# A linear-attention and GEGLU block in f32: how the first two tiles of x are loaded, and when the masks are made

## The chip, the cores and the metric

One core of a Trainium2 chip runs the whole kernel. The metric is the device time in microseconds (us) of one execution; the time of a version is the median of its runs.

## The reference

One block over a sequence of 2048 rows of width 576, all in f32. `x` is normalized by rows; the normalized rows go into a linear attention with 32 heads of 18 and into a gated feed-forward net of width 4608; the two results are multiplied and added to `x`.

```python
def block(x, wqkv, wo, w_gate, w_up, w_down):
    xn = (x - mean(x)) / sqrt(var(x) + 1e-5)
    q, k, v = heads(xn @ wqkv)                    # 32 heads of 18
    phi = lambda t: where(t > 0, t + 1, exp(t)) + 1e-6
    kv = einsum("bhsd,bhse->bhde", phi(k), v)     # over all rows
    z = phi(k).sum over s
    o = einsum(phi(q), kv) / (einsum(phi(q), z) + 1e-6)
    s = o @ wo
    h = gelu(xn @ w_gate) * (xn @ w_up)
    return x + s * silu(h @ w_down)
```

## The kernel before

The 2048 rows are 16 tiles of 128, in 4 blocks (`TB`) of 4 tiles (`TT`). A value of f32 is split into two fp32r words: ACT copies it to fp32r (the high word), and DVE or POOL subtracts that copy from the value (the low word). A product in full precision is then several passes of TensorE (PE) over words: `KV_PASSES` has seven for each of the two halves of the 576 columns.

The work in order: k and v (and the last columns of q) for all tiles, with `kv` summed up in PSUM; q; the normalizer and the attention's output matrix; then gate and up by blocks of columns; last the down product. From the second block of 8 tiles on, `x` comes in already transposed and is normalized in that form. The first four tiles are loaded with rows on partitions, normalized and transposed on PE.

The opening goes by a hand-written order, since `pin` keeps instructions of each engine as the program has them (helpers `act`, `vec`, `mm`, `pool`, `dma`; a line such as L90 or L87 in the profile is that of a helper). Calls on `nc.gpsimd` that are not pinned may be moved by the scheduler.

- `turn_idle(n, v)`: n transposes of `ident` (or of a small value, once that is there) into the PSUM tile `idle`, whose contents nobody reads. They stand at the beginning and in the gaps of the opening.
- `load_x(n, k, eng)`: a load of k row tiles of `x` into `x_n`, on SP's queue, or on that of `eng`. One tile is 384 KB.
- `load_kv(c, j)`: a piece of the k and v weights into `rw`, on SP's queue: 624 KB, or 576 KB for c = 2.
- `spread(n, k)`: the moments of a tile: on DVE two `bn_stats`, one `bn_aggr` and an addition, on ACT a Ln and an Exp. `scales(n)`: three small operations on DVE. `center(n)`: DVE subtracts the mean and multiplies by the scale, 128x768 in one instruction.
- `turn(n)`: six transposes of the normalized tile on PE, three for each half j, into the PSUM tiles `xt`. `place(n, js, words)`: ACT rounds `xt` into the operand `xo_B` (word 0), DVE writes the remainders (word 1).
- `kv_hi`, `kv_lo`: the two words of a weight piece into `wkv`, by ACT and by POOL or DVE. `x_mm(t, c, passes)`: the passes of tile t and weight piece c.

Two loads stand at the head of the queues: tile 0 on SP's, tile 1 on ACT's. Behind tile 0, SP's queue has the weight pieces and tiles 2 and 3. `make_masks` writes three things into `small`: `mask` and `maskh`, by `affine_select` on POOL, and `zc`, of which rows 64 to 127 are zeroed by a memset. It is called after tile 5 of the first pass. Its instructions are not pinned; in the program the scheduler has put the memset of `zc` ahead of the select that makes `ident`, and the others where the call stands. `mask`, `maskh` and `zc` are first read behind the sixteenth tile, at about 187 us.

Of the kernel before, what the change touches and what calls it, by code (L numbers as in the profile page):

```python
# [10 lines left out]
AF = mybir.ActivationFunctionType  # L11
ALU = mybir.AluOpType
# [3 lines left out]
P = 128  # L16
# [3 lines left out]
H = 32  # L20
DH = D // H
# [4 lines left out]
TT = TBN // P  # L26
NG = DF // (2 * P)
HG = 7
GW = HG * DH
NHG = 5  # L30
# [5 lines left out]
Q4 = 64  # L36
# [19 lines left out]
def block_kernel(ctx, tc, x, xe, xt_d, wq_d, wkv0_d, wkv1_d, wkv2_d, wo, wgu_d, wd_d, out):  # L56
    nc = tc.nc
# [11 lines left out]
    def big(i, shape, dt, name):  # L69
        return sb.tile(shape, dt, tag=f"b{i}", bufs=1, name=name)  # L70
# [10 lines left out]
    def tmp(shape, name):  # L81
        return sb.tile(shape, F32, tag="tmp", bufs=4, name=name)
# [3 lines left out]
    def act(*args, **kw):  # L86
        pin(nc.scalar.activation(*args, **kw))  # L87

    def vec(op, *args, **kw):
        pin(getattr(nc.vector, op)(*args, **kw))  # L90
# [4 lines left out]
    def pool(op, *args, **kw):  # L95
        pin(getattr(nc.gpsimd, op)(*args, **kw))  # L96

    def dma(out, in_, eng=None):
        tc.keep_in_program_order((eng or nc.sync).dma_start(out=out, in_=in_))
# [9 lines left out]
    small = sb.tile([P, 640], F32, name="small")  # L109
# [9 lines left out]
    def load_x(n, k, eng=None):  # L119

        if n % 2 == 0:
            xstat[n // 2] = big(14 + n // 2 % 2, [P, 12 * P], F32, f"x_{n}")
        if n < TT:
            o = x_of(n)[:, None] if k == 1 else xstat[n // 2][:, 0 : 12 * P].rearrange(
                "p (t j d) -> p t j d", t=2, j=2)
            dma(out=o, in_=xe[n * P : (n + k) * P].rearrange("(t p) j d -> p t j d", p=P), eng=eng)
        else:
            dma(
                out=xstat[n // 2][:, 0 : 2 * D].rearrange("p (t d) -> p t d", t=2),
                in_=x[n * P : (n + 2) * P].rearrange("(t p) d -> p t d", p=P),  # L130
            )

    def x_of(n):

        w = 6 * P if n < TT else D
        return xstat[n // 2][:, n % 2 * w : (n % 2 + 1) * w].rearrange("p (j d) -> p j d", j=2)
# [24 lines left out]
    def scales(n0):  # L161

        n, mv, st = mom.pop(n0)
        far = n0 >= TT
        v, r, c = (st[:, i, 0:n] for i in range(1, 4))
        if n == 1:
            vec("tensor_scalar", c, r, r, -0.5, op0=ALU.mult, op1=ALU.mult)
            vec("tensor_scalar", c, c, v, 1.5, op0=ALU.mult, op1=ALU.add)
            vec("tensor_scalar", c, c, r, None, op0=ALU.mult)
        else:  # L170
            vec("scalar_tensor_tensor", c, r, -0.5, r, op0=ALU.mult, op1=ALU.mult)
            vec("tensor_mul", c, c, v)
            o = mv[:, 0:n, 1] if far else c
            vec("scalar_tensor_tensor", o, c, 1.5, r, op0=ALU.add, op1=ALU.mult)
        if far:
            mom[n0] = mv
            return
        for t in range(n):
            scale_of[n0 + t] = mv[:, t, 0:1], c[:, t : t + 1]

    def center(n):

        xs = x_of(n)
        m, r = scale_of.pop(n)
        vec("tensor_scalar", xs, xs, m, r, op0=ALU.subtract, op1=ALU.mult)

    def spread_out(n):

        mr[n] = bank(f"mr_{n}")
        mv = mom.pop(n)  # L190
        for t in range(2):
            for q in range(2):
                o = mr[n][:, (2 * t + q) * P : (2 * t + q + 1) * P]
                pin(nc.tensor.transpose(o, mv[:, t, q : q + 1].to_broadcast([P, P]), ident))

    def norm(n, js=(0, 1)):

        tb, t = divmod(n, TT)
        s, b = divmod(tb, 2)
        v = mr[n].rearrange("p (t q c) -> p t q c", t=2, q=2)  # L200
        for j in js:
            f = xf[s][BS[b][j]][:, :, t * P : t * P + P2].rearrange("p k (t c) -> p k t c", t=2)
            for q, op in enumerate(("tensor_sub", "tensor_mul")):
                vec(op, f, f, v[:, None, :, q, :].to_broadcast([P, 3, 2, P]))
# [38 lines left out]
    mom, scale_of, xts, mr = {}, {}, {}, {}  # L243
# [54 lines left out]
    def load_kv(c, j):  # L298
        n = KV.index((c, j))
        if n % 2 == 0:  # L300
            raws["kv", n // 2] = big((2, 3, 12)[n // 2], [P, 2, 3, CW[c]], F32, f"rw_{n}")
        raws[c, j] = raws["kv", n // 2][:, n % 2]
        dma(out=raws[c, j], in_=wkv_d[c][j])
# [28 lines left out]
    def load_q(j):  # L332
        raws["q", j] = big(12, [P, 2, 3, Q2], F32, f"rq_{j}")
        dma(out=raws["q", j], in_=wq_d[:, j].rearrange("c p k f -> p c k f"))

    def prep_q(c, j):
        raw, main = raws["q", j][:, c], wq[j]
        cs, r = slice(c * Q2, (c + 1) * Q2), slice(2 * KR, 3 * KR)
        act(main[:, 0:3, cs], raw, AF.Copy)
        for o, src, hi in (  # L340
            (main[:, 3, cs], raw[:, 0, :], main[:, 0, cs]),
            (wq_l[:, j, cs], raw[:, 1, :], main[:, 1, cs]),
            (main[r, 2, cs], raw[r, 2, :], main[r, 2, cs]),
        ):
            pool("tensor_sub", o, src, hi.bitcast(F32))
# [183 lines left out]

    at = {}  # L530

    def band(m, src, pattern, c):
        nc.gpsimd.affine_select(
            out=m, in_=src, compare_op=ALU.is_ge, fill=0.0, base=0,
            pattern=[[-s, n] for s, n in pattern], channel_multiplier=c,
        )
        nc.gpsimd.affine_select(
            out=m, in_=m, compare_op=ALU.is_ge, fill=0.0, base=DH - 1,
            pattern=[[s, n] for s, n in pattern], channel_multiplier=-c,
        )  # L540

    def make_masks():
        ones = tmp([P, NHG * H], "ones")
        nc.gpsimd.memset(ones, 1.0)

        at["mask"] = mask = small[:, 0:GW]
        m3, o3 = (i.rearrange("p (h j) -> p h j", h=HG) for i in (mask, ones[:, 0:GW]))
        nc.gpsimd.affine_select(
            out=m3, in_=o3, compare_op=ALU.is_ge, fill=0.0, base=-1,
            pattern=[[-DH, HG], [0, DH]], channel_multiplier=1,  # L550
        )
        nc.gpsimd.affine_select(
            out=m3, in_=m3, compare_op=ALU.is_ge, fill=0.0, base=DH,
            pattern=[[DH, HG], [0, DH]], channel_multiplier=-1,
        )
        nc.gpsimd.memset(mask[0:1, :], 1.0)
        at["maskh"] = small[:, P : P + NHG * H].rearrange("p (g h) -> p g h", g=NHG)
        band(at["maskh"], ones.rearrange("p (g h) -> p g h", g=NHG), [[-GW, NHG], [DH, H]], 1)
        at["zc"] = small[:, P + NHG * H : P + 2 * NHG * H].rearrange("p (g h) -> p g h", g=NHG)
        nc.gpsimd.memset(at["zc"][Q4:P], 0.0)  # L560

    def kv_done():

# [561 lines left out]
    def turn_idle(n, v=None):  # L1125
        src = ident if v is None else v.to_broadcast([P, P])
        for _ in range(n):
            pin(nc.tensor.transpose(idle[:, 0:P], src, ident))

    turn_idle(20)  # L1130
    load_x(0, 1)
    load_kv(0, 0)
    load_x(1, 1, nc.scalar)
    load_kv(0, 1)
    load_kv(1, 0)
# [6 lines left out]
    spread(0, 1)  # L1142
    turn_idle(2, mom[0][1][:, 0, 0:1])
    scales(0)
    turn_idle(4, scale_of[0][1])
    center(0)
    turn(0, lambda n: (own_bank if n[-1] == "0" else bank)(n))
    turn_idle(3)
# [64 lines left out]
    def x_next(n):  # L1213

        spread(n, 2)
        scales(n)

    def form(nm, tb, j):

        o = build(0, nm, 12)  # L1220
        load_turned(tb, j)
        keep(0, nm, o)
# [19 lines left out]
    for n in range(3, 2 * TT):  # L1242
        early, middle, ends, after = [], [], [], []
        if n == 3:
            early += [lambda: spread_out(4), lambda: norm(4)]
        if n == 3:
            after.append(lambda: x_next(6))
        if n == 4:
            middle.append(lambda: spread_out(6))
            after.append(lambda: norm(6))  # L1250
        if n >= TT:
            j, c = divmod(n - TT, 2)
            prep_q(c, j)
            if n == TT + 1:
                load_q(1)
        if n == 5:
            after.append(lambda: x_next(8))
        if n == 6:
            after += [lambda i=i: difference(0, i) for i in range(2)]
        if n == 7:  # L1260
            ends.append(lambda: difference(0, 2))
            after.append(lambda: form("T1", 2, 0))
        kv_tile(n, early, middle, ends, after)
        if n in (4, 5):
            load_x(2 * n, 2)
        if n == TT:
            for nm in BS[0]:
                keep(0, nm, xo[0][nm])
        if n == TT + 1:
            make_masks()  # L1270
        if n == TT + 3:
            keep(0, "B22", xo[0]["B22"])

# [87 lines left out]
    for q in range(NQ):  # L1361
        g = q // 2
# [72 lines left out]
```

## Time and profile before

| what | value |
|---|---|
| median of 3 runs | 1493.03 us (1492.82 to 1493.14) |
| profiled execution | 1492.64 us |
| its span, first to last instruction | 1490.9 us |
| mean granted clock of TensorE | 0.999 |
| PE busy | 1482.9 us, 99% of the span |
| DVE, ACT, POOL busy | 1062.4, 563.4, 549.4 us |
| DMA | 260.67 MB, mean 175 GB/s |

Times in the views are from the span's start. "PE" is TensorE's matmuls (transposes too), "PEld" its weight loads; "SPq" and "ACTq" are the sequencers of SP and ACT that issue DMAs. In the chain and in the timeline a row has start, duration, engine or DMA, and what; in brackets stands how long the engine was idle before and what ended that. A row with "x6" is a group of six.

### The profile page before, as it was taken

To read this page: it belongs to the slowest core of one execution; us is meant where nothing else is said; L and a number is where in the kernel's file an instruction comes from. 1 tells how busy PE (TensorE), PEld (TensorE's weight loads), DVE (VectorE), ACT (ScalarE), POOL (GpSimd) and SP (SyncE) were. 2 spreads that over 40 slices of the span, in tenths; PEclk is the share of its full clock that TensorE was granted. 3 is DMA by queue.
4 is the path that set the end of the run, shared out by engine and by line. 5 is a ranking of instruction groups with operands and counts; after the bars stand their busy time and mean duration, and the time that the engine had idled before them with its cause. 6 is when DMAs were issued, how large, how long until landed. Compare 5 with 4: busy or idle time off the path is not lost.

```text
span 1490.9 us, 22327 instructions
## 1 busy us (share of the span) xinstructions
PE 1482.9 (99%) x8355; PEld 1328.2 (89%) x8355; DVE 1062.4 (71%) x1582; ACT 563.4 (38%) x1047; POOL 549.4 (37%) x521
## 2 busy tenths in 40 slices
PE   9999999999999999999999999999999999999998
PEld 8989989988888888888888888888899999999998
DVE  7678467377788787788787778787785575555775
ACT  5444455332232232332222322223445454445443
POOL 5453431144665544565554565554310020001120
PEclk9999999999999999999999999999999999999999
DMA  6355015533443423344433344333697666686873
GB/s 238 131 198 194 1 45 191 207 149 136 161 173 145 161 107 132 148 174 157 152 121 122 142 173 171 139 136 117 218 334 256 227 217 222 226 290 218 299 254 112
DMA packets 114614, 260.67 MB, mean 175 GB/s; under 512 B 10234, under 2 KB 38778, under 8 KB 112458
## 3 DMA queue, kind: packets, MB, share of 16 engines
q1 hardware_dynamic: 112730, 249.95, 46.7%
q0 software_dynamic: 1632, 8.91, 1.6%
q8 instruction: 65, 1.06, 0.3%
q10 hardware_dynamic: 144, 0.39, 0.1%
q14 instruction: 43, 0.35, 0.1%
HBM read 161.27 MB, written 97.91 MB: 174 GB/s over the span
## 4 chain that ended last, share of the span: by engine, by line
PE 95%; DVE 2%; DMA 1%; ACT 1%; POOL 0%; issue 0%; SPq 0%; DVEq 0%; ACTq 0%; POOLq 0%
PE bd L1010 27%; PE al L804 15%; PE ga L804 15%; PE de L804 15%; PE be L804 8%; PE kv L93 7%; PE s L93 4%; PE q L93 2%; PE kv_a L93 1%; DMA kept_T<-xo_T 1%; DMA xf_B<-in_xt_dram 0%; PE d L93 0%; PE kw L93 0%; DVE xf_B L90 0%; PE b L93 0%
## 5 line engine op out<-in xcount | busy, mean ns | idle before, releaser
L1010 PEld LDWEIGHTS bd<-t,s 128*128 128x128 f32 x3024 | 400.9, 188 | 0.1
L1010 PE MATMUL bd<-t,s 128*128 128x288 f32 x3024 | 401.0, 295 | 0.0
L90 DVE TENSOR_TENSOR s<-sr,s 128x512 fp32r<-128x512 f32 x252 | 176.4, 738 | 119.6 <-ACT s L87 110.1
L87 ACT ACTIVATE s<-sr 128x512 fp32r<-128x512 f32 x252 | 149.2, 625 | 189.6 <-PE bd L1010 133.6
L96 POOL TENSOR_TENSOR hs<-h,h 128x512 f32<-128x512 f32 x68 | 94.7, 1402 | 202.7 <-DVE h L90 200.0
L87 ACT ACTIVATE h<-h 128x512 f32<-128x512 f32 x108 | 67.1, 633 | 244.3 <-POOL sm L96 123.1
L96 POOL TENSOR_TENSOR sx<-sx 128x288 f32<-128x288 f32 x24 | 27.8, 1180 | 322.9 <-DVE sx L90 321.9
L93 PE MATMUL kv<-wkv,xo_B 128*128 128x416 f32 (+1 forms) x672 | 129.2, 349 | 0.3 <-DVE xo_B L90 0.2
L93 PEld LDWEIGHTS kv<-wkv,xo_B 128*128 128x128 f32 x672 | 121.6, 188 | 2.1 <-DVE xo_B L90 0.5
L96 POOL TENSOR_TENSOR sm<-raw 128x384 f32<-128x384 f32 x72 | 75.7, 1051 | 108.8 <-DMA raw<-in_wgu_dram 87.9
L90 DVE TENSOR_TENSOR wa<-raw,wa 128x256 fp32r<-128x256 f32 x72 | 79.0, 1098 | 51.6 <-ACT wa L87 50.5
L90 DVE TENSOR_TENSOR h<-h,u 128x512 f32<-128x512 f32 x108 | 95.7, 886 | 3.7
L87 ACT ACTIVATE wa<-sm 128x1152 fp32r<-128x1152 f32 x36 | 41.8, 1161 | 135.2 <-PE de L804 135.2
L96 POOL TENSOR_TENSOR td<-td 128x288 f32<-128x288 f32 x72 | 71.5, 993 | 50.9 <-DMA td<-in_wd_dram 46.6
L90 DVE TENSOR_TENSOR wa<-sm,wa 128x768 fp32r<-128x768 f32 x72 | 62.9, 874 | 36.9 <-ACT wa L87 36.0
L90 DVE TENSOR_TENSOR wb<-raw,wb 128x256 fp32r<-128x256 f32 (+1 forms) x108 | 72.0, 666 | 7.2 <-ACT wb L87 5.6
L90 DVE TENSOR_TENSOR wb<-sm,wb 128x256 fp32r<-128x256 f32 x72 | 61.5, 855 | 20.6 <-ACT wb L87 20.0
L87 ACT ACTIVATE u<-al 128x512 f32<-128x512 f32 x72 | 40.8, 593 | 88.4 <-PE al L804 88.4
L90 DVE TENSOR_TENSOR u<-u,ga 128x512 f32<-128x512 f32 x72 | 49.3, 686 | 19.8 <-PE ga L804 19.2
L804 PE MATMUL al<-xo_B,wa 128*128 128x512 f32 x252 | 63.0, 389 | 0.0
L804 PE MATMUL be<-xo_T,wa 128*128 128x512 f32 x252 | 63.0, 389 | 0.0
L804 PE MATMUL be<-xr_T,wa 128*128 128x512 f32 x252 | 63.0, 389 | 0.0
(175 smaller groups left out, 2779.1 us busy)
## 6 DMA issues: line engine op xcount, KB each, us to landing
sr<-hs SPq DMA_DIRECT2D x252, 256.0 KB
hs<-h SPq DMA_DIRECT2D x68, 512.0 KB
raw<-in_wgu_dram SPq DMA_DIRECT2D x36, 768.0 KB
hs<-hs SPq DMA_DIRECT2D x102, 256.0 KB
td<-in_wd_dram SPq DMA_DIRECT2D x18, 576.0 KB
td<-td SPq DMA_DIRECT2D x18, 576.0 KB
tr<-td SPq DMA_DIRECT2D x16, 576.0 KB
tr<-in_wd_dram SPq DMA_DIRECT2D x12, 576.0 KB
```

What stands on the lines that cost most here:

```text
L87: pin(nc.scalar.activation(*args, **kw))
L90: pin(getattr(nc.vector, op)(*args, **kw))
L93: pin(nc.tensor.matmul(*args, **kw))
L96: pin(getattr(nc.gpsimd, op)(*args, **kw))
L804: nc.tensor.matmul(o, w[0:rows, wi, :], xop[0:rows, xi, :], start=(start and n == 0), stop=(n == len(PASSES) - 1), skip_group_check=True,)
L1010: nc.tensor.matmul(banks[j][:, 0:HALF], hw[n, s][:, a, t * P : (t + 1) * P], w[:, c, g % 4], start=(new and g == 0 and m == 0), stop=(g == ...
```

## The change

The load of tile 1 still stands on ACT's queue, but `make_masks` now stands ahead of it, at the beginning, all of its instructions pinned. The zeros of `zc` are no longer a memset: ACT makes them as Relu of minus the mask `maskh`, which is 0 or 1. So on ACT's queue the load of tile 1 stands behind that Relu, which waits for POOL's fourth select, and tile 0's load is the only one issued at first, followed by SP's weight pieces. The order of the selects differs too: the two of `mask`, then the two of `maskh`, where the scheduler had them interleaved. POOL makes `ones` where the memset of `zc` was, ahead of the select of `ident`. `center(0)` becomes two instructions of 128x384, and the transposes of the first half wait only for the first. Four of the fillers go: 18 for 20 at the beginning, 2 for 4 behind the scale of tile 0. Nothing of this work is left at tile 5. The other engines' orders are the same as before.

```diff
 def center(n):
     xs = x_of(n)
     m, r = scale_of.pop(n)
-    vec("tensor_scalar", xs, xs, m, r, op0=ALU.subtract, op1=ALU.mult)
+    for o in [xs] if n else [xs[:, j] for j in range(2)]:
+        vec("tensor_scalar", o, o, m, r, op0=ALU.subtract, op1=ALU.mult)
...
-    def band(m, src, pattern, c):
...
+    def select(o, src, base, pattern, c):
+        pool(
+            "affine_select",
+            out=o, in_=src, compare_op=ALU.is_ge, fill=0.0, base=base,
+            pattern=pattern, channel_multiplier=c,
+        )

     def make_masks():
         ones = tmp([P, NHG * H], "ones")
-        nc.gpsimd.memset(ones, 1.0)
+        pool("memset", ones, 1.0)
...
-        nc.gpsimd.memset(at["zc"][Q4:P], 0.0)
+        m, o = (i.rearrange("p (h j) -> p h j", h=HG) for i in (mask, ones[:, 0:GW]))
+        select(m, o, -1, [[-DH, HG], [0, DH]], 1)
+        select(m, m, DH, [[DH, HG], [0, DH]], -1)
+
+        two = small[:, P : P + 2 * NHG * H].rearrange("p (i g h) -> p i g h", i=2, g=NHG)
+        at["maskh"], at["zc"] = m, zc = two[:, 0], two[:, 1]
+        select(m, ones.rearrange("p (g h) -> p g h", g=NHG), 0, [[GW, NHG], [-DH, H]], 1)
+        select(m, m, DH - 1, [[-GW, NHG], [DH, H]], -1)
+        pool("memset", mask[0:1, :], 1.0)
+
+        act(zc[Q4:P], m[Q4:P], AF.Relu, scale=-1.0)
...
-    turn_idle(20)
+    turn_idle(18)
     load_x(0, 1)
     load_kv(0, 0)
+    make_masks()
     load_x(1, 1, nc.scalar)
     load_kv(0, 1)
...
     scales(0)
-    turn_idle(4, scale_of[0][1])
+    turn_idle(2, scale_of[0][1])
     center(0)
...
-        if n == TT + 1:
-            make_masks()
```

More of the change, by code (lines that the diff above doesn't have):

```diff
@@ L530, in block_kernel @@
     at = {}
-    def band(m, src, pattern, c):
[L533 to L539, printed above, removed]
+    def select(o, src, base, pattern, c):
[3 more added lines that the diff above has]
+            pattern=pattern, channel_multiplier=c,
         )
@@ L543, in make_masks @@
         ones = tmp([P, NHG * H], "ones")
-        nc.gpsimd.memset(ones, 1.0)
+        pool("memset", ones, 1.0)
         at["mask"] = mask = small[:, 0:GW]
[L547 to L560, printed above, removed]
+        m, o = (i.rearrange("p (h j) -> p h j", h=HG) for i in (mask, ones[:, 0:GW]))
[7 more added lines that the diff above has]
+        act(zc[Q4:P], m[Q4:P], AF.Relu, scale=-1.0)
     def kv_done():
```

## The prediction

> **What bounds the kernel now.** I read the page's busy times and chain first, then the chain of waits of the first 30 us, then busy time by stretch.
>
> ```profile
> PE 1482.9 (99%) x8355; PEld 1328.2 (89%) x8355; DVE 1062.4 (71%) x1582; ACT 563.4 (38%) x1047; POOL 549.4 (37%) x521
> ...
> PE 95%; DVE 2%; DMA 1%; ACT 1%; POOL 0%; issue 0%; SPq 0%; DVEq 0%; ACTq 0%; POOLq 0%
> ```
>
> PE is the chain almost everywhere. An edit of the first microseconds can therefore only do one thing: let the dense PE work begin earlier or later. The chain of the opening says what that beginning hangs on:
>
> ```profile
> 0.81 3.94 DMA x<-in_xe_dram
> 4.77 0.83 DVE bn L90 x2
> ...
> 12.27 0.50 ACT xo_B L87
> 12.79 0.42 DVE xo_B L90
> ...
> 24.32 0.88 PE xt L213 x6
> ```
>
> And the stretches (us, then busy us and count of PE, PEld, DVE, ACT, POOL, then granted clock, DMA share, GB/s):
>
> ```profile
> 7.60:12.80 5.20, 5.20 (x36) 4.38 (x34) 4.17 (x14) 2.94 (x8) 4.80 (x3) 1.00 1.01 415
> 12.80:24.30 11.50, 11.24 (x61) 10.80 (x59) 11.01 (x22) 6.93 (x13) 8.77 (x7) 1.00 0.72 271
> ```
>
> From 12.8 to 24.3 us PE (11.24 of 11.50) and DVE (11.01) are both full, and both begin there with the second tile: its transposes, ACT's rounding copy (12.27), DVE's remainders (12.79). So the end of the kernel moves by as much as the second tile is ready earlier or later. That is the quantity to work out. Before 12.8 much of PE's time is its filler transposes into `idle`, which cost nothing as long as data is late.
>
> **First tile's load, alone.** Now both x loads are issued together, and the four weight loads follow on SP's queue:
>
> ```profile
> 0.81 0.39 SPq L99 DMA_DIRECT2D x<-in_xe_dram  x1
> 0.83 0.39 ACTq L99 DMA_DIRECT2D x<-in_xe_dram  x1
> ```
>
> Bytes by stretch, same columns as above:
>
> ```profile
> 1.50:3.00 1.50, 1.25 (x6) 1.25 (x7) 0.00 (x0) 0.58 (x1) 0.20 (x1) 1.00 0.63 219
> 3.00:3.50 0.50, 0.50 (x4) 0.50 (x3) 0.00 (x0) 0.00 (x0) 0.00 (x0) 1.00 0.96 369
> 3.50:4.00 0.50, 0.50 (x5) 0.50 (x4) 0.00 (x0) 0.00 (x0) 0.00 (x0) 1.00 1.05 423
> 4.00:4.50 0.50, 0.50 (x4) 0.50 (x3) 0.00 (x0) 0.00 (x0) 0.00 (x0) 1.00 1.07 433
> ```
>
> and by queue (q1 is SP's, q10 ACT's), for 1.5 to 3.1 us and then for 3.0 to 4.6 us:
>
> ```profile
> q1 hardware_dynamic: 75, 0.23, 39.4%
> q10 hardware_dynamic: 45, 0.14, 26.2%
> ...
> q1 hardware_dynamic: 124, 0.41, 63.3%
> q10 hardware_dynamic: 99, 0.26, 41.4%
> ```
>
> An x tile is 384 KB, 0.39 MB. Summing the stretches, 0.33 MB are over by 3.0, 0.51 by 3.5, 0.73 by 4.0, 0.94 by 4.5, and at that rate 1.15 by 5.0. SP's queue alone passes 0.39 MB near 3.7 (0.23 by 3.1, then 0.26 a us), and DVE starts on it at 4.77; the lag from last byte to DVE is thus at most 1.05 us, and 0.6 if it counts from where both tiles' 0.79 MB are over, near 4.15. If SP's queue gets all bytes, 0.39 MB are over at 3.2 and DVE starts at 3.8 to 4.25, 0.5 to 0.95 us earlier. I take 3.85, a gain of 0.9, since the two queues moved side by side and ended close together.
>
> ACT and POOL in the timeline:
>
> ```profile
> 5.93 0.29 ACT L87 ACTIVATE st<-mv,eps_t 128x1 f32<-128x1 f32 x1 [3.85 <-DVE mv L90]
> 6.38 1.24 ACT L87 ACTIVATE wkv<-rw 128x1248 fp32r<-128x1248 f32 x1
> 7.70 3.21 POOL L96 TENSOR_TENSOR wkv<-rw,wkv 128x832 fp32r<-128x832 f32 x2 [6.00 <-ACT wkv L87]
> ...
> 30.16 0.24 ACT L87 ACTIVATE w_q<-w_q 128x64 f32<-128x64 f32 x1
> ```
>
> The first weight piece (624 KB, 0.64 MB) is then over at 1.03 MB, 4.7, and usable by 5.3 on the same lag; ACT reaches it at 6.38 - 0.9 = 5.5, so it is only just covered; uncovered, it would take from the 0.9 that POOL's `wkv` (7.70) is to start earlier, of which I count 0.2 at most.
>
> [...]
>
> **Second tile's load, behind the zeros.** POOL's timeline:
>
> ```profile
> 1.10 0.23 POOL L560 MEMSET small<- 64x160 f32 x1
> 1.41 0.29 POOL masks.py:199 TENSOR_SCALAR_AFFINE_SELECT ident<-ident 128x128 f32<-128x128 f32 x1
> ...
> 61.91 0.34 POOL L548 TENSOR_SCALAR_AFFINE_SELECT small<-ones 128x126 f32<-128x126 f32 x1
> 62.21 0.50 POOL L533 TENSOR_SCALAR_AFFINE_SELECT small<-ones 128x160 f32<-128x160 f32 x1
> 62.66 0.37 POOL L552 TENSOR_SCALAR_AFFINE_SELECT small<-small 128x126 f32<-128x126 f32 x1
> 62.98 0.51 POOL L537 TENSOR_SCALAR_AFFINE_SELECT small<-small 128x160 f32<-128x160 f32 x1
> ...
> 64.62 1.41 POOL L96 TENSOR_TENSOR pk<-pk,e_k 128x576 f32<-128x576 f32 x1 [0.99 <-DVE pk L90]
> ```
>
> In the program `ones` takes the place of the old memset of `small` ahead of POOL's `ident` select (both 0.23 us), so PE's fillers start at 1.75 as before; four selects of the masks follow, in an order where each waits for the one before. That is 1.70 + 0.34 + 0.37 + 0.50 + 0.51 = 3.42. So ACT's new Relu can start near 3.5; it takes some 0.3 (64x160; the 128x64 row has 0.24), and the load is issued at 3.5 to 3.8 instead of 0.83. The first loads' bytes begin 0.7 to 1.2 after their issue (0.81 and the stretch from 1.5), so these begin at 4.2 to 5.0; I take 4.6. From then on ACT's queue shares with weights: it had 0.26 of 0.67 MB from 3.0 to 4.6, 39%; between that and a half, of 0.42 MB a us, 0.39 MB take 1.9 to 2.4 us. Over at 6.5 to 7.0, with the lag of 0.6 to 1.05 usable by DVE at 7.1 to 8.05. I take 7.5.
>
> What stands behind the Relu on ACT: the x load, then the first tile's Ln, which comes at 5.93 - 0.9 = 5.0, so nothing else is held up. POOL's `wkv` remainder, first behind the masks, waits for ACT and does not start before 7.70 - 0.9 = 6.8; the masks end before 4. Taking the mask work out of 61.9 to 63.5 is worth nothing: POOL idles 0.99 us right after it, for DVE.
>
> **From there to the dense part.**
>
> ```profile
> 7.25 0.68 DVE L90 TENSOR_SCALAR x<-x,mv,st 128x768 f32<-128x768 f32 x1
> 7.84 0.81 DVE L90 BATCH_NORM_STATS2 bn<-x 128x6 f32<-128x288 f32 x2
> ...
> 9.89 0.72 DVE L90 TENSOR_SCALAR st<-st 128x1 f32<-128x1 f32 x3
> 10.64 0.68 DVE L90 TENSOR_SCALAR x<-x,mv,st 128x768 f32<-128x768 f32 x1
> ...
> 11.74 0.82 PE L213 MATMUL xt<-ident,x 128*128 128x128 f32 x6
> ...
> 10.96 0.19 PEld L93 LDWEIGHTS kv<-wkv,xo_B 128*128 128x128 f32 x1 [0.24 <-POOL wkv L96]
> ...
> 1.75 4.53 PE L1128 MATMUL idle<-ident 128*128 128x128 f32 x20 [1.75 <-POOL ident masks.py:199]
> ```
>
> DVE runs from 7.84 to 11.32 without a wait, in a fixed order, so the second tile's centering moves one for one with the start of its `bn`. Now that start waits only for DVE, which was busy with the first tile's centering. After the change the first tile is centered at 7.25 - 0.9 = 6.35, in two halves of 0.34 to 0.46 each (half of 0.68, and at most half of the 0.72 / 3 = 0.24 that one of 128x1 takes), so DVE is free at 7.1, earlier than the load is usable. So `bn` starts at 7.5, 0.34 us earlier, and the wait "DVE for DMA x" takes the place of "DVE for DVE". PE, moreover, transposed the second tile at 11.74 though it was centered at 11.32: it stood behind a matmul at 10.96, which had waited 0.24 for POOL's `wkv`. That POOL work starts 0.9 earlier with ACT's rounding of the weights, so up to 0.2 more can come out. Gain 0.34 to 0.55; I take 0.4. The halves let the first three transposes start some 0.3 sooner, which only widens the first tile's lead, worth nothing at the end. Fewer fillers (18+2+2 for 20+2+4) cost nothing while the first tile comes 0.9 earlier: at 0.21 each (4.53 over 20, with a tail) the first 20 end near 6.3, the last two wait for the scale at about 6.3 and end at 6.8, and the transposes begin at 6.7 to 6.8.
>
> Sum: the profiled execution took 1492.64 us, its span 1490.9; less 0.4 that is 1492.24. The median of the runs is 1493.03, 0.39 above the profiled one, so I forecast **1492.6**.
>
> **Rivals.** Times are by the median.
>
> *The second load is late* (slower). Mechanism: ACT's queue gets under 39% or the issue slips behind POOL. It decides once `bn` of tile two starts after 8.0 (7.84 plus the 0.15 to 0.2 that POOL's wait leaves). At a share of 25%, 0.39 MB take 3.7 us, and `bn` starts at 4.6 + 3.7 + 0.6 = 8.9: 0.9 lost. Half of that is the middle: 1493.4. For it: the upper end of my own estimate is 8.05; against: four terms would have to be at their ends. 18%.
>
> *The second load is in time.* At 7.1 DVE goes straight on: 0.75 plus 0.2, so 1492.0 to 1492.3. For it: the lower end, 7.1. 15%.
>
> *The change does nothing*: the first tile's load already passes first, and the second is no hindrance to it. Then `bn` stays at 4.77, DVE is free at 8.0, tile two is in by 7.5 to 8.05: 1493.1. The queue rows speak against it, 3%; the case also stands for a head start that DVE or POOL eat before 24.3, 4%: 7%. [...]
>
> *The clock stays slow longer* (slower).
>
> ```profile
> 7.26 0.79 PE L1128 MATMUL idle<-ident,st 128*128 128x128 f32 x4 [0.56 <-DVE st L90]
> ...
> L1128 PE MATMUL idle<-ident,st x4: 272/290/466, 7.3 to 7.8; 128*128 128x128 f32 x4
> L1128 PE MATMUL idle<-ident,mv x2: 421/421/421, 6.1 to 6.3; 128*128 128x128 f32 x2
> ```
>
> Fillers took 421 ns up to 6.3 and 272 from about 7.6: PE got fast there. If fewer fillers left PE idle, this could come later; the 36 matmuls of 7.6 to 12.8 took 5.20 us; at 421 for 272 ns they would take 2.9 more, of which fillers and waits hide a part: 1 to 2.5 us, 1494.0 to 1495.5. Against it: with the first tile earlier PE's idle 0.56 before 7.26 shrinks. 5%.
>
> [...]
>
> **How the numbers follow.** Forecast 55%, the rivals 18, 15, 7 and 5. The forecast's own range is 1492.2 to 1492.9. For 8 in 10 I take in the early and the late load and a scatter of 0.3 between executions: 1491.7 to 1494.0; most of the clock case is left out. Within 0.2% (3.0 us, about what a measurement of this kernel can tell from no change) lies everything but the far end of the clock case and what I did not think of: 95%. Faster by over 3 us would need more than the whole wait for the first load: 2%; slower 3%.
>
> **What would show it.** In the profile after: the first `bn` at 3.8 to 4.25 instead of 4.77; ACT's x load issued at 3.5 to 3.8; the second pair of `bn` at 7.1 to 8.05, released by DMA x and not by DVE; the second tile's transposes near 11.3; the six near 24.32 at about 23.9. A second `bn` after 8.0, or 421 ns matmuls after 8 us, would make the prediction wrong in sign; a `bn` at 7.1 wrong in size. If 24.3 moves and the end does not, something between absorbs the head start.

## The result, and the profile after

| kernel | median, us | range | runs | ratio to before (95%) |
|---|---|---|---|---|
| before | 1493.07 | 1492.54 to 1493.41 | 16 | |
| after | 1496.18 | 1494.01 to 1497.46 | 16 | 1.0019 [1.0011, 1.0027] |

The changed kernel is slower by 3.1 us, 0.2%. The forecast was 1492.6 with a range up to 1494.0. The profiled execution of after took 1496.28 us, its span is 1494.5 (before 1492.64 and 1490.9), so the two traces differ by as much as the medians, and the trace can be read for the cause.

The page of after: busy times, and the chain by engine.

```profile
PE 1483.2 (99%) x8351; PEld 1329.5 (89%) x8351; DVE 1062.7 (71%) x1583; ACT 563.9 (38%) x1048; POOL 548.2 (37%) x520
...
PE 98%; DMA 0%; DVE 0%; ACT 0%; issue 0%; POOL 0%; DVEq 0%; ACTq 0%; POOLq 0%
```

PE's busy time is the same within 0.3 us although the span is 3.6 longer: the difference shows as idle PE. (That busy time holds slower matmuls as well is seen below; what they add is offset by the fillers at the beginning, 18 for 20, which took 3.50 us for 4.53.) The chain of waits of the opening of after (start, duration, what) has it:

```profile
2.97 0.01 ACT small L87
2.98 7.26 DMA x<-in_xe_dram
...
10.26 0.83 DVE bn L90 x2
...
11.51 0.34 DVE xo_B L90
...
11.90 1.75 PE kv L93 x4
...
28.86 0.66 PE xt L214 x6
```

Before, the chain ran over the *first* tile's load, which DVE had at 4.77. Now it runs over the *second* tile's: issued at 2.98, on the chain for 7.26 us. The step that was to gain did gain, and nothing came of it. The timeline of after:

```profile
1.59 3.50 PE L1123 MATMUL idle<-ident 128*128 128x128 f32 x18 [1.59 <-POOL ident masks.py:199]
...
2.98 0.37 ACTq L99 DMA_DIRECT2D x<-in_xe_dram  x1
...
3.66 0.82 DVE L90 BATCH_NORM_STATS2 bn<-x 128x6 f32<-128x288 f32 x2 [3.66 <-DMA x<-in_xe_dram]
...
6.07 0.87 DVE L90 TENSOR_SCALAR x<-x,mv,st 128x384 f32<-128x384 f32 x2
...
10.26 0.82 DVE L90 BATCH_NORM_STATS2 bn<-x 128x6 f32<-128x288 f32 x2 [3.33 <-DMA x<-in_xe_dram]
...
11.43 0.73 DVE L90 TENSOR_TENSOR xo_B<-xt,xo_B 128x256 fp32r<-128x256 f32 x2
...
11.90 1.75 PE L93 MATMUL kv<-wkv,xo_B 128*128 128x416 f32 x4 [3.42 <-DVE xo_B L90]
```

Tile 0 is there 1.1 us earlier (3.66 for 4.77), but DVE waits 3.33 us for tile 1 and starts on it at 10.26 instead of 7.84. On DVE tile 0's remainders `xo_B` stand behind the second `bn` in the program and ran behind it (11.43 after 10.26); so PE, which has tile 0's high words long before, waits 3.42 us for its low words.

What the load did in those 7 us, by queue (packets, MB, share), from 2.98 to 6.40 us, where ACT's queue (q10) has no row, and from 6.4 to 9.9:

```profile
q1 hardware_dynamic: 294, 1.30, 97.7%
...
q1 hardware_dynamic: 229, 1.04, 73.2%
q10 hardware_dynamic: 144, 0.39, 29.2%
```

For 3.4 us after its issue the load moved nothing, while SP's queue moved 1.30 MB: two weight pieces of 0.64 MB. Then it had a good quarter of the bytes, 0.39 of 1.43 MB.

The third part is the clock. Busy time by stretch of after, then one row of before (busy and count of PE, PEld, DVE, ACT, POOL, then granted clock, DMA share, GB/s):

```profile
8.00:9.00 1.00, 0.48 (x3) 0.16 (x2) 0.00 (x0) 0.07 (x1) 0.92 (x2) 1.00 1.04 412
9.00:10.00 1.00, 0.00 (x0) 0.00 (x0) 0.00 (x0) 0.00 (x0) 0.88 (x1) 1.00 1.03 425
10.00:11.00 1.00, 0.00 (x0) 0.00 (x0) 0.74 (x2) 0.00 (x0) 0.00 (x0) 1.00 1.01 411
11.00:12.00 1.00, 0.10 (x1) 0.10 (x1) 0.90 (x5) 0.61 (x3) 0.00 (x0) 0.58 1.05 429
12.00:18.00 6.00, 6.00 (x22) 5.43 (x23) 3.35 (x11) 2.65 (x4) 3.33 (x2) 0.50 0.54 219
```
```profile
12.00:18.00 6.00, 6.00 (x36) 5.87 (x34) 5.04 (x13) 4.96 (x7) 4.63 (x4) 1.00 0.99 371
```

After PE's idle 3.4 us the granted clock is halved at about 11.2 (0.58 over the stretch from 11 to 12) and stays at 0.50 until 18: PE does 22 matmuls in 6 us where it did 36. The dense work of tile 1, which began at 12.81, begins at 17.39, 4.6 us later. Its first rows in the timelines, of before and then of after:

```profile
12.81 11.22 PE L93 MATMUL kv<-wkv,xo_B 128*128 128x416 f32 x59
```
```profile
17.39 3.91 PE L93 MATMUL kv<-wkv,xo_B 128*128 128x416 f32 x18
```

The six transposes that stood at 24.3 come at 28.7, 4.4 later; the end is 3.6 later. From these transposes on PE is idle for 5.4 us in both traces, and busy for 0.8 us less in after; the traces don't show why.

### The profile page after: what moved, and what is told of

It is laid out like the page before. It is cut to its first block, busy times and chain, and to the rows that moved or that the text cites. A ratio compares the mean times of both kernels' runs of the same rounds, so it can differ in the third digit from the quotient of the medians.

```text
span 1494.5 us, 22319 instructions
## 1 busy us (share of the span) xinstructions
PE 1483.2 (99%) x8351; PEld 1329.5 (89%) x8351; DVE 1062.7 (71%) x1583; ACT 563.9 (38%) x1048; POOL 548.2 (37%) x520
## 4 chain that ended last, share of the span: by engine, by line
PE 98%; DMA 0%; DVE 0%; ACT 0%; issue 0%; POOL 0%; DVEq 0%; ACTq 0%; POOLq 0%
PE bd L1005 27%; PE al L799 15%; PE ga L799 15%; PE de L799 15%; PE kv L93 8%; PE be L799 8%; PE s L93 4%; PE q L93 3%; PE kv_a L93 1%; DMA x<-in_xe_dram 0%; PE d L93 0%; PE kw L93 0%; PE b L93 0%; PE mr L195 0%; PE xt L214 0%
## 5 line engine op out<-in xcount | busy, mean ns | idle before, releaser
L799 PE MATMUL al<-xr_B,wa 128*128 128x512 f32 x252 | 63.0, 389 | 0.0
L799 PE MATMUL ga<-xr_T,wa 128*128 128x512 f32 x252 | 63.0, 389 | 0.0
```

The costliest lines, as they stand in the source:

```text
L799: nc.tensor.matmul(o, w[0:rows, wi, :], xop[0:rows, xi, :], start=(start and n == 0), stop=(n == len(PASSES) - 1), skip_group_check=True,)
```

## The experiments

All kernels are the kernel after with the edit shown, unless they say otherwise. The table gives for each the start of the second `bn` on tile 1 and of the dense part (the matmuls that stood at 12.81 before) in its profiled run, and the median. The kernel before, run beside each of them, had medians of 1493.04 to 1493.15 us.

| kernel | bn of tile 1 | dense part | median, us (runs) | ratio to before (95%) |
|---|---|---|---|---|
| before | 7.84 | 12.81 | 1493.07 (16) | |
| after | 10.26 | 17.39 | 1496.18 (16) | 1.0019 [1.0011, 1.0027] |
| e1_load_first | 7.94 | 13.45 | 1493.27 (11) | 1.0001 [0.9992, 1.0011] |
| e2_sp_third | 8.86 | 14.62 | 1494.76 (11) | 1.0008 [0.9999, 1.0017] |
| e3_fillers | 9.93 | 16.05 | 1494.63 (11) | 1.0012 [1.0003, 1.0020] |
| e4_issue_2us | 7.04 | 13.22 | 1492.96 (11) | 0.9999 [0.9990, 1.0008] |
| e5_sp_third_whole | 6.99 | 11.96 | 1491.84 (11) | 0.9992 [0.9983, 1.0001] |
| e6_whole | 10.23 | 16.41 | 1495.72 (11) | 1.0017 [1.0008, 1.0026] |
| e7_tile0_first | 10.37 | 15.08 | 1494.99 (11) | 1.0014 [1.0005, 1.0023] |
| e8_thirds | 9.36 | 14.84 | 1495.08 (11) | 1.0011 [1.0002, 1.0020] |
| e9_all_behind | 11.03 | 17.75 | 1497.32 (7) | 1.0027 [1.0016, 1.0038] |
| e10_sp_second_whole | 6.83 | 14.97 | 1495.89 (11) | 1.0018 [1.0009, 1.0027] |
| e11_before_sp_third | 7.00 | 11.98 | 1492.30 (11) | 0.9994 [0.9985, 1.0003] |
| e12_maskh_first | 9.93 | 16.09 | 1495.40 (11) | 1.0014 [1.0005, 1.0023] |

A straight line through the fourteen rows gives 0.81 us of the median for each us of the start of the dense part, with 0.5 us of scatter around it; with the times of the profiled runs themselves in place of the medians it gives 0.88. So the prediction's first step, that the end goes as the dense part begins, holds within a fifth. Only e10 stands more than a microsecond off the line, 1.2 above it.

**Is it the late load, or the rest of the change?** e1 issues the load where it was, keeps masks at the beginning, Relu, halves and fewer fillers:

```diff
-    make_masks()
     load_x(1, 1, nc.scalar)
+    make_masks()
     load_kv(0, 1)
```

> The changed kernel with one thing undone: tile 1's load is issued on ACT's queue at the beginning again, ahead of the masks and zeros; masks, halves and 18+2 fillers stay. Theory (the late load is the whole cause): its bytes begin near 2.1 us as before, the second pair of bn starts at 7.8 and the time is that of before, 1492.7 to 1493.3. Rival (the early masks, the halves or the fewer fillers cost something by themselves): above 1494, with the second bn still near 7.8.

Measured 1493.27. Its timeline:

```profile
4.74 0.82 DVE L90 BATCH_NORM_STATS2 bn<-x 128x6 f32<-128x288 f32 x2 [4.74 <-DMA x<-in_xe_dram]
...
7.94 0.81 DVE L90 BATCH_NORM_STATS2 bn<-x 128x6 f32<-128x288 f32 x2
```

The first `bn` is back at 4.74, the second has no wait, and the loss is gone. The masks, the Relu, the halves and the fillers together cost 0.2 us, which can't be told from nothing, though one of its eleven runs took 1495.42 (in the profiled run PE's first matmuls on `kv`, from 9.53 on, still took 1.04 us for two, where before took 0.65, and the dense part began 0.6 later; that is the clock rival's case, and in this run it cost no more than this). The place of the load is the cause.

**Is it the clock?** e3 fills PE's wait with 28 more transposes that nobody reads:

```diff
     x_mm(0, 0, of((0, HI[:2])))
-    turn_idle(1)
+    turn_idle(29)
```

> The changed kernel with 28 fillers more on PE behind the first two matmuls of tile 0, where PE waited from 8.5 to 11.9 us; the load stays late. Clock theory (the wait lets the granted clock fall to half for 6.8 us, and that costs about half of the loss and all of the scatter): no 421 ns matmuls after 12 us, mean granted clock 0.999 or more in all runs, 1494.0 to 1494.8 with a spread under 1 us. Rival (the late second tile alone costs the 3 us): 1495.5 to 1497 as it is.

Measured 1494.63, 1.55 below after. Busy time by stretch of e3:

```profile
8.00:12.00 4.00, 3.05 (x26) 3.00 (x27) 2.84 (x8) 1.44 (x4) 1.74 (x2) 1.00 1.03 419
12.00:16.00 4.00, 4.00 (x32) 3.84 (x31) 1.88 (x6) 1.18 (x3) 3.10 (x2) 1.00 0.77 315
```

The clock stays full though tile 1 is about as late as in after (9.93), and the dense part begins 1.34 us earlier, of 4.58 lost. By the medians half of the loss of 3.1 us is the clock, by this profile some 30%; the two kernels' intervals overlap, and the fillers ran until 13.1, past the end of the wait, so the clock's part is rather more than the profile has it. The runs of after itself point the same way: the two with a mean granted clock of 1.000 took 1494.01 and 1494.51, the seven with 0.997 took 1495.60 to 1497.41. The rest is the wait itself. One part of the expectation failed: the runs of e3 still scatter from 1493.78 to 1496.65, with a clock of 0.999 or 1.000 in ten of the eleven, so the clock is not the whole of the scatter.

**Must tile 0's work stand behind the wait?** e7 puts tile 0's remainders and the second weight piece's rounding ahead of tile 1's moments:

```diff
-    spread(1, 1)
     place(0, (0,), (1,))
+    kv_hi(0, 1)
+    place(0, (1,), (1,))
+    spread(1, 1)
     scales(1)
     center(1)
-    kv_hi(0, 1)
...
     x_mm(0, 0, of((1, HI[:2])))
-    place(0, (1,), (1,))
```

> The changed kernel with one thing moved: what tile 0 needs (its remainders on DVE, the second weight piece's rounding on ACT) stands ahead of tile 1's moments, so that neither waits behind the late load. Order theory (PE stood from 8.5 to 11.9 us because tile 0's remainders were queued behind tile 1's bn on DVE): PE works on tile 0 in that time, the dense part begins about 14.5 instead of 17.4, the granted clock mostly stays up, 1493.8 to 1495. Rival (tile 1 is needed whatever comes first): 1495.5 to 1497.

Measured 1494.99, 1.2 below after, with overlapping intervals. Of e7's waits of PE from 9 to 15 us (us, times, longest), the longest:

```profile
PE xt L214 <- DVE x L90: 2.6, 1, 2.6
```

PE now has tile 0's work from 7.8 to 11.1 and then stands for tile 1; the clock still falls, for 3.4 us (14.6 to 18.0) instead of 6.8. So the order on DVE (and of the weight piece on ACT, which the edit moves too) seems to make it worse, but any order has to wait for the load.

**Why did the load wait?** Three theories: a fixed delay; its place in the order of loads (a turn for each load on each queue); the bytes queued ahead of it on SP's queue. e4 issues it early by letting the Relu read `ones`, which are there sooner than the selects. Relu of minus one is zero as well.

```diff
-        act(zc[Q4:P], m[Q4:P], AF.Relu, scale=-1.0)
+        act(zc[Q4:P].rearrange("p g h -> p (g h)"), ones[Q4:P], AF.Relu, scale=-1.0)
```

> The changed kernel with the zeros made from POOL's ones instead of the fourth select, so that ACT's Relu and the load behind it start when the table load is over, at 2.1 us instead of 2.97. Order theory (its bytes begin once the weight pieces that were issued ahead are through): only one weight piece is far ahead, bytes begin at 4.5 to 5.1, go at 38% of the rate and are over near 7.6; second bn at 8.0, 1493.0 to 1493.8. Rival (the queue is slow: 6.9 us from issue to the end, as in the changed kernel, whatever lies ahead): over at 9.0, second bn at 9.3, 1494.5 to 1496.

Measured 1492.96. It went out earlier than I meant, at 1.25, before the Relu can have run, as the table load on ACT lasts until 2.08. So it tests another case than was meant:

```profile
1.25 0.39 ACTq L99 DMA_DIRECT2D x<-in_xe_dram  x1
...
6.45 1.25 ACT L87 ACTIVATE wkv<-rw 128x1248 fp32r<-128x1248 f32 x1 [0.97 <-DMA rw<-in_wkv_dram]
...
7.04 0.81 DVE L90 BATCH_NORM_STATS2 bn<-x 128x6 f32<-128x288 f32 x2
```

Now tile 0's load passes alone and tile 1's shares with the first weight piece alone (62% and 41% by queue from 3.0 to 5.6 us). Tile 1 is in time, but the weight piece isn't: ACT waits 0.97 us for it, POOL's remainder of it comes later, and 0.8 us that tile 1 gained come to nothing at 13.22.

e8 cuts the second weight piece into three loads of 208 KB, so that its third has one place but a third of the bytes:

```diff
-        dma(out=raws[c, j], in_=wkv_d[c][j])
+        if (c, j) == (0, 1):
+            for k in range(3):
+                dma(out=raws[c, j][:, k], in_=wkv_d[c][j][:, k])
+        else:
+            dma(out=raws[c, j], in_=wkv_d[c][j])
```

> The changed kernel with the second weight piece loaded in three DMAs of 208 KB instead of one of 624 KB; tile 1's load is issued at 2.97 us as it was. Theory of places (a load on the other queue begins once the DMA in service and the next one, already taken, are through, whatever their size): its bytes begin at 4.8 to 5.6 instead of 6.45, the second bn starts at 7.3 to 8.2, 1492.8 to 1494. Rival (a fixed delay or a fixed amount of bytes ahead): they begin near 6.5, bn after 9, 1495 to 1497.

Measured 1495.08; the load's bytes begin at 6.30 for 6.45. Its queues from 2.98 to 6.25 us, where q10 has no row:

```profile
q1 hardware_dynamic: 487, 1.17, 100.7%
```

The theory of turns, which had the bytes begin at 4.8 to 5.6, falls: by 6.5 us all rows of the first two thirds had begun and 71 of the last one's 128, but only 6 of the load's 128.

e9 leaves only tile 0 and the first weight piece on SP's queue, and puts all the rest behind tile 1 on ACT's:

```diff
...
     load_x(1, 1, nc.scalar)
-    load_kv(0, 1)
+    load_kv(0, 1, nc.scalar)
...
-    load_x(3, 1)
+    load_x(3, 1, nc.scalar)
...
```

> Measures the late load by itself: the changed kernel with all loads after tile 1's put behind it on ACT's queue, so that at its issue, 2.97 us, SP's queue holds only tile 0 and the first weight piece, 1.03 MB, through at about 4.7 to 5.1. Its total time is not of interest, since ACT spends 3 us issuing. Backlog theory (the load waits for bytes that SP's queue has had ahead): its bytes begin at 4.2 to 5.1 and it is over by 6, with the DMA engines busy throughout. Rival (a fixed 3.4 us from issue to first byte on ACT's queue): they begin at 6.4 and the DMA engines stand idle from 5.1 to 6.4.

Its queues, from 2.98 to 4.60 us and from 4.6 to 6.0:

```profile
q1 hardware_dynamic: 165, 0.69, 105.1%
...
q10 hardware_dynamic: 168, 0.51, 96.3%
q1 hardware_dynamic: 23, 0.04, 6.6%
```

The same issue at 2.98, but the bytes begin at 4.69, as the one piece ahead ends, and then nearly all the engines' time goes to ACT's queue. So there is no fixed delay: it is the bytes ahead. The kernel as a whole is slower still, 1497.32, since ACT issues loads until 7.2 before it can do tile 0's Ln.

e12 issues the load 0.7 us earlier, by an order of masks in which the two selects that the Relu needs come first:

```diff
-        select(m, o, -1, [[-DH, HG], [0, DH]], 1)
-        select(m, m, DH, [[DH, HG], [0, DH]], -1)
...
         select(m, ones.rearrange("p (g h) -> p g h", g=NHG), 0, [[GW, NHG], [-DH, H]], 1)
         select(m, m, DH - 1, [[-GW, NHG], [DH, H]], -1)
+        act(zc[Q4:P], m[Q4:P], AF.Relu, scale=-1.0)
...
+        select(m, o, -1, [[-DH, HG], [0, DH]], 1)
+        select(m, m, DH, [[DH, HG], [0, DH]], -1)
         pool("memset", mask[0:1, :], 1.0)
-
-        act(zc[Q4:P], m[Q4:P], AF.Relu, scale=-1.0)
```

> The kernel after with the two selects of maskh, and the Relu that reads them, ahead of the two of mask: the load of tile 1 is issued near 2.25 us instead of 2.98, 0.45 us behind the issue of the second weight piece (1.8) and ahead of that of the third. Theory A, all that is issued on SP's queue before the load passes first: the bytes still begin near 6.3, the second pair of bn starts near 10, and the time stays near 1496. Theory B, only what was issued well over half a microsecond earlier is ahead (in the kernel after the second piece was issued 1.2 us before the load and was ahead, the third 0.6 us before it and was not): the bytes begin when the first piece is through, 4.5 to 5.1, the load shares with the second piece and is over at 6.7 to 7.2, the second pair of bn starts at 7.3 to 8, and the time is 1492.5 to 1493.5, or 1494 to 1495 where the second half of the centering meets POOL's wkv and takes 2.2 us.

Measured 1495.40. Of its timeline, and of its queues from 2.29 to 6.10 us, where q10 has no row:

```profile
2.29 0.38 ACTq L99 DMA_DIRECT2D x<-in_xe_dram  x1
...
9.93 0.82 DVE L90 BATCH_NORM_STATS2 bn<-x 128x6 f32<-128x288 f32 x2 [2.79 <-DMA x<-in_xe_dram]
```
```profile
q1 hardware_dynamic: 364, 1.46, 99.6%
```

Theory A's numbers: 0.7 us at the issue are worth 0.3 at the data. It waits for the whole of the second piece even when that was issued only half a microsecond before. What exactly counts as ahead stays open: in after the third piece was also issued before the load, and its bytes passed beside the load's and not ahead. Age doesn't decide it: that piece was issued at 2.19, 0.8 us before the load, and the second piece of e12, which was ahead, only 0.6 before. After e8 an amount of bytes is likelier than a number of loads; no run tried it.

**Where should it stand?** e2 puts it third on SP's queue, between the two weight pieces:

```diff
-    load_x(1, 1, nc.scalar)
+    load_x(1, 1)
     load_kv(0, 1)
```

> The changed kernel with tile 1's load on SP's queue, third behind tile 0 and the first weight piece, and no longer behind the zeros. Theory (bytes are served in the order of issue, and the changed kernel's load was late because two weight pieces had been issued ahead of it): 0.39 + 0.64 + 0.39 = 1.43 MB are over at about 5.7 us, the second bn starts when DVE is free, at 7.0, and the time is 1492.0 to 1492.6. Rival (any load beside the weight pieces is slow, whichever queue): second bn after 8, 1493.3 or more.

Measured 1494.76: a miss, though tile 1 was in time. DVE's instructions on `x` and POOL's on `wkv` in e2 (durations in ns, min/median/max, then starts):

```profile
L90 DVE TENSOR_SCALAR x<-x,mv,st x3: 482/679/2196, 6.3 to 11.5; 128x384 f32<-128x384 f32 x2, 128x768 f32<-128x768 f32 x1
```
```profile
L96 POOL TENSOR_TENSOR wkv<-rw,wkv x3: 1065/1939/2277, 6.8 to 11.7; 128x832 fp32r<-128x832 f32 x2, 32x416 fp32r<-32x416 f32 x1
```

The first half of the centering took 482 ns, the second 2196: it ran from 6.74 to 8.93, POOL's first `wkv` from 6.78 to 8.72. It ended 0.21 us behind POOL's 1939 ns, and the first half had lasted until 6.82, so POOL was at work when the second could begin. DVE thus seems to have been held until POOL had ended; by what, the trace doesn't show. PE, without work again, lost the clock (0.57 from 9 to 13 us). e3, e8 and e9 show the same 2.2 us, the other five profiled kernels with the halves don't; in e3 and e8 the late load covered it.

e5 is e2 with the halves undone, so that the centering is over or well begun before POOL starts:

```diff
-        for o in [xs] if n else [xs[:, j] for j in range(2)]:
-            vec("tensor_scalar", o, o, m, r, op0=ALU.subtract, op1=ALU.mult)
+        vec("tensor_scalar", xs, xs, m, r, op0=ALU.subtract, op1=ALU.mult)
```

> Tile 1's load third on SP's queue, and the first tile centered in one instruction instead of two halves. With the halves and this load, the second half took 2.20 us instead of 0.47: it began 0.04 us before POOL's first wkv remainder and ended just after it. Port theory (a DVE instruction of this kind that meets a POOL one waits for its end, and the halves put a second start at just that time): in one piece it begins 0.4 us ahead of POOL and takes 0.7, the second bn starts at 7.0, and the time falls to 1491.8 to 1492.8. Rival (the 2.2 us are chance of that execution and cost nothing in the median): 1494 to 1495, as with the halves.

Measured **1491.84**, the best of all: 4.3 us below after. Against before its interval, 0.9983 to 1.0001, just takes in no gain. Its timeline:

```profile
3.99 0.82 DVE L90 BATCH_NORM_STATS2 bn<-x 128x6 f32<-128x288 f32 x2 [3.99 <-DMA x<-in_xe_dram]
...
6.39 0.68 DVE L90 TENSOR_SCALAR x<-x,mv,st 128x768 f32<-128x768 f32 x1
6.83 3.21 POOL L96 TENSOR_TENSOR wkv<-rw,wkv 128x832 fp32r<-128x832 f32 x2 [3.75 <-ACT wkv L87]
6.99 0.81 DVE L90 BATCH_NORM_STATS2 bn<-x 128x6 f32<-128x288 f32 x2
...
11.96 5.75 PE L93 MATMUL kv<-wkv,xo_B 128*128 128x416 f32 x29
```

The centering in one piece began 0.44 us before POOL and took its 0.68; the second `bn` follows without a wait, and the dense part begins 0.85 us before that of before. This is about the gain that the change's first half was worth.

e6 undoes the halves alone (e5's edit), the load where after has it:

> The changed kernel with only the halves undone: the first tile is centered in one instruction. The load stays late, at about 10 us. Load theory (what costs is the late load and the clock): no change, 1495.5 to 1497. Rival (the halves are part of the loss, by meeting POOL): 1494.5 or less.

Measured 1495.72, and the second `bn` at 10.23: with the load late, the halves don't matter.

e11 is the kernel *before* with tile 1 third on SP's queue and nothing else:

```diff
-    load_x(1, 1, nc.scalar)
+    load_x(1, 1)
```

> The kernel before with one word gone: tile 1's load is on SP's queue, third, instead of on ACT's; masks at tile 5, centering whole, 20+2+4 fillers as they were. Theory (all that can be gained here is tile 0's load alone, with tile 1's not late): first bn at 4.0, second at 7.0, 1491.7 to 1492.2. Rival (the early masks or the fewer fillers are part of the gain): 1492.5 or more.

Measured 1492.30, 0.1 above the range of its theory, the dense part at 11.98, as e5. The gain, if the interval (0.9985 to 1.0003) is not all of it, is the loads' alone; the masks have no part in it that the two intervals could show. e10 is e5 with tile 1 second on SP's queue, ahead of the first weight piece:

```diff
     load_x(0, 1)
+    load_x(1, 1)
     load_kv(0, 0)
     make_masks()
-    load_x(1, 1)
```

> Tile 1's load second on SP's queue, straight behind tile 0 and ahead of the first weight piece; the first tile centered in one instruction. Tile 0 is usable at 4.0 us as with the load in third place, tile 1 long before 7; the first weight piece is over at 1.43 MB, 5.7 us, usable at 6.2 instead of 5.5, so POOL's first remainder ends 0.6 later and with it the matmul before tile 1's transposes. Theory (in third place the weight piece's remainder on POOL and DVE's chain are in balance): 0.3 to 0.7 slower than third place, 1492.1 to 1492.6. Rival (the weight piece has slack): the same as third place, 1491.8.

Measured 1495.89, a miss of both theories. ACT in its timeline, then busy time and bytes by stretch in e10, then in e5:

```profile
8.27 1.24 ACT L87 ACTIVATE wkv<-rw 128x1248 fp32r<-128x1248 f32 x1 [2.82 <-DMA rw<-in_wkv_dram]
```
```profile
6.00:7.00 1.00, 0.84 (x4) 0.32 (x3) 0.96 (x3) 0.00 (x0) 0.00 (x0) 1.00 0.89 305
```
```profile
6.00:7.00 1.00, 0.43 (x2) 0.19 (x2) 0.93 (x4) 0.75 (x1) 0.17 (x1) 1.00 0.94 379
```

The first weight piece is what came late: ACT waits 2.82 us for it, and everything behind it follows. It landed on the first of the 16 engines at 5.7 us and on the last at 7.7, where in e5 these stand 0.5 apart, and the rate was lower, 305 for 379 GB/s from 6 to 7. Why, isn't settled.

## Why the prediction was wrong, point by point

- **What bounds the opening: right.** The end moved with the start of the dense part, 0.8 for 1 (table).
- **First tile's load, alone: right in its mechanism.** Predicted `bn` at 3.85, range 3.8 to 4.25; it came at 3.66, a little below the range, and at 3.71 to 3.99 in the other runs with a lone first tile.
- **The selects and the issue: better than forecast.** Predicted 3.5 to 3.8; it was 2.98. The rows I summed, 0.34 to 0.51 us, are from 62 us on; at the beginning the same selects took 0.33 to 0.35, and the first began at 1.49.
- **"The first loads' bytes begin 0.7 to 1.2 after their issue, so these begin at 4.2 to 5.0": this step failed.** They began 3.5 us after the issue, at 6.45. The rows I took it from are those of loads with nothing ahead of them; here two weight pieces stood on the other queue. I had priced the *sharing* of two queues that start together, and not the *waiting* of one that starts behind 1.3 MB. e9 (one piece ahead: 1.7 us from issue to bytes), e12 and after (two: 3.8 and 3.5) and e4 (tile 0 ahead: 1.8) show it. So `bn` started at 10.26 where 7.5 was forecast, and a gain of 0.4 became, with the fall of the clock (below), a loss of 3.1.
- **"39% … between that and a half … 1.9 to 2.4 us": mis-sized.** It was 27% of the bytes and 3.2 us, nearer to the rival's 25% and 3.7. The lag to DVE, 0.6, was right (last byte at 9.69, `bn` at 10.26). The sum also dropped half of its own range: it goes on from 4.6 alone, and from 5.0 its upper end is not 8.05 but 8.45, past the 8.0 at which the rival was to be decided.
- **The rival "the second load is late"** named the outcome and its point of decision (`bn` after 8.0), at 18%, and half of the mechanism: of its two conditions the low share came (27%), the late issue didn't, and the wait for the first byte was in neither. Its price was wrong: I gave 0.9 us of delay at most and half of that as its time, 1493.4. The delay was 2.4.
- **The rival "the clock stays slow longer"** came in as its consequence. I had taken it for a separate case, through fewer fillers, at 1494.0 to 1495.5; the clock came down because PE waited 3.4 us. So the two cases were not alternatives: the late load brought the clock down with it (0.50 from 12 to 18 us), and the 3.1 us measured are the sum of both, of which e3 gives the clock a third to a half, and the runs of after at full clock rather more than half.
- **"Before 12.8 much of PE's time is its filler transposes, which cost nothing as long as data is late": incomplete.** They cost nothing, but fillers kept the clock up in e3 (1.00 from 8 to 16 us, where in after it was 0.50 from 12 to 18), and e3 shows what they are then worth.
- **"DVE runs … in a fixed order, so the second tile's centering moves one for one": right, but I followed only tile 1 down that order.** Tile 0's remainders stand behind the second `bn` in it, so a late tile 1 stops tile 0's work too.
- **"The halves … worth nothing at the end": right in after** (e6), wrong in e2, where the load is in time and the second half meets POOL: there they cost 2 to 3 us (e2 against e5). In e1, with the load in time too, the two didn't meet.

The sign came out wrong for these reasons, and both marks that the prediction gave for it came: a second `bn` after 8.0, and slow transposes after 8 us (0.42 us for one at 14.44). Yet the difference is only about as large as the 0.2% below which I had put 95%.

## What to carry to other kernels

The load that was put on a second queue didn't get its share from its issue on: up to two whole pieces, 1.3 MB in after, passed before its first byte. So count the bytes already queued on the other queue, and put a load where its turn is right on one queue rather than behind an instruction on another: third in e5 and e11, while second, in e10, cost 2.8 us. When an early wait leaves PE without work, price the clock with it: here it fell after waits of 1.6 us (e2, e8) to 3.4 us (after). And look at what else stands in the waiting engine's order behind the wait. An instruction cut in two begins twice, and either start can meet another engine's work: in four of the nine profiled kernels with the halves the second one met POOL's `wkv` and took 2.2 us for 0.47.

## What the runs showed of the hardware

- **A queue behind a backlog.** From issue to first byte: 1.3 us for the load of tile 1 in before (0.83 to 2.11), 3.5 in after, 1.7 with one weight piece ahead in e9. It began when the one or two pieces ahead were through, not with a turn of its own; the third and fourth piece, issued 0.8 and 0.3 us before it in after, were not ahead.
- **ACT's sequencer issued a load while the engine loaded its table**: at 1.25 in e4, where the table load lasted from 0.80 to 2.08 and the Relu ahead of the load in the program ran at 2.09.
- **The clock fell in whole steps, and for longer than the wait.** In after it is half from 11.2 to 18, 6.8 us, behind a wait of 3.4; in e7 and e12 for 3.4, half of that, behind waits of 2.6 and 2.9. Take stretches of 3.41 us (the clock's first three records in after, full, half and full, last 6.83, 6.83 and 1474.56 us: 2, 2 and 432 of them), counted from the time at which the granted clock rose: in the fourteen profiled runs each of the 21 falls (the one at the end of every run among them) comes behind a stretch in which PE was busy for at most 1.58 us (e8, at 9.55), and no other stretch has less than 1.84 (e10, from 7.44). After's runs scatter over 3.5 us where before's scatter over 0.9. Whether the place of the wait among these stretches makes that scatter wasn't tried, and e3, with hardly a fall of the clock, scatters over 2.9.
